# Linear attention and a two-layer MLP on one core: the preparation of the first batch is redistributed over GpSimd, VectorE and the first-layer blocks

## The chip, the core and the metric

The kernel runs on one core of a Trainium2 chip. A core has TensorE (PE, matrix products into PSUM), VectorE (DVE), ScalarE (ACT), GpSimd (POOL) and SyncE (SP, which here only issues transfers). Each engine takes its own instructions strictly in program order; GpSimd also issues the transfers that turn float32 into bf16 on the way. The metric is the device time of one execution in microseconds (us), the median of several runs.

## The reference, cut to what matters

```python
q_s = softmax over the 64 features of q;  k_s = softmax over the 576 positions of k
kv  = einsum('bhsd,bhse->bhde', k_s, v)            # 64 x 64 for each head
attn = einsum('bhsd,bhde->bhse', q_s, kv)          # 8 batches, 8 heads, 576 positions, 64 features
x = attn.transpose(0, 2, 1, 3).reshape(4608, 512)
h = x @ w_in                                       # 512 -> 2048
out = maximum(0.01 * h, h) @ w_out                 # 2048 -> 512
```

All inputs and the output are float32.

## The kernel before, in words

**Layout.** The 576 positions of a head are 64 partitions times R = 9 rows, and two heads' halves fill 128 partitions, so that a batch is a tile [128, 4, 9, 64] of `q`, `k` or `v` (HL = 4 pairs of heads; pairs 0 and 1 are called H0, pairs 2 and 3 H1). The exponentials are written as bf16 (`qe`, `ke`); v is cast to bf16 into `vb`, with a column of ones that gives the sum of k's exponentials. The product of ke and vb is `pkv`; scaled and masked it becomes `kd`, four blocks g = 0 to 3. Blocks 0 and 2 come from gg = 0 (H0), blocks 1 and 3 from gg = 1 (H1). q's exponentials are divided by their sums (`q_norm`), transposed on TensorE (`q_transpose`) and copied out of PSUM (`q_keep`) into `qT`; `attend` multiplies by kd and casts the result into `xT`, which holds x transposed in four blocks of 128 features. Row r of q gives the 64 columns from 64 r of a batch.

**The MLP.** The 4608 tokens go in nine tiles of 512. For a tile, layer 1 makes 16 units j (128 hidden features each), each with four matmuls over xT's blocks in the order 0, 2, 1, 3 (`layer1`, line 456); `leaky` (line 467) on ScalarE takes them out of PSUM into `gj`. Layer 2 (`layer2`, line 478) adds up the 16 units over four sub-tiles of 128 tokens. In tile 0 layer 1 is cut in two halves of 256 columns, two units to a PSUM bank, and layer 2 runs unit by unit, four matmuls each.

**The order.** The tile framework schedules nothing by itself here: the program's text is the order on every engine. Work of a later batch is hung in by hand: `at(t, u, ...)` puts functions behind unit u of tile t, and `run(t, u)` calls them. In tile 0 the numbers 0 to 31 are the layer-1 units of the two halves, and from 32 on the units of layer 2; so (0,41) is behind unit 9 of layer 2. PSUM has eight banks: six in the pool `psB` (units, transposes, products, all under one tag) and two in `psO`. A bank is free again when the last reader of its former tile is done.

**The start, batch 0** (lines 515 to 576). SyncE issues q's rows 0 to 3 (RA), k in two halves, v in two halves, and q's rows 4 to 8. GpSimd waits with a one-column copy into `gate` for k's second half, then issues the first half of w_in (units 0 to 7) in four pieces, first the two of gg = 0 (blocks 0 and 2), then the two of gg = 1. `q_first` takes q's first four rows with 16 small exponentials on ScalarE. k's maximum over all positions is found with VectorE and TensorE (`k_tree`, `k_max_pe`, `k_all_dve`, `k_all_pe`) and subtracted by VectorE (`k_sub_ps`, line 362). ScalarE does k's exponentials (line 203) and both casts of v (line 213). GpSimd issues w_in's second half (line 133) behind another gate, at line 542. Then follow `kv_pair` for H0 and H1, the transposes, and `attend`. Matmuls on zeros (`wake`, line 324) keep TensorE busy in between. Rows 4 and 5 (R1) and rows 6 to 8 (R2) of q follow in layer 1, with hooks at units 3 to 17.

**Batch 1.** `hold_sync(0, ...)` makes SyncE wait for the first piece of w_in's second half and then issues k (two halves), q and v of batch 1. GpSimd waits at line 572 for k's first half and issues w_out in five pieces; `hold_sync(1, ...)` waits for w_out's units 8 to 11 and lets batch 2's loads go. The hooks of unit 15 find k's maximum on VectorE (`k_tree` line 162, `k_allmax` to line 187) and subtract it (line 195): H0 on GpSimd, H1 on VectorE. q's maximum (line 226) is subtracted on GpSimd (line 256, rows RA = 0 to 3 and RB = 4 to 8), its exponential is on ScalarE (line 264), sum and division on VectorE (lines 273 and 280). `kv(1)` stands at (0,41).

Of the kernel before, what the change touches and what calls it, by code (L numbers as in the profile page):

```python
# [25 lines left out]
def kernel(  # L26
# [57 lines left out]

    ALLH, ALLR = slice(0, HL), slice(0, R)
    RA, RB = slice(0, 4), slice(4, R)
    R1, R2 = slice(4, 6), slice(6, R)
    st = [{} for _ in range(B)]


# [58 lines left out]
    def k_tree(b, hs, steps=slice(0, 4)):  # L149
        n = hs.stop - hs.start  # L150
        ks = st[b]["k"][:, hs]
        if steps.start == 0:
            st[b]["t4"] = mx_pool.tile([P, HL, 4, D], FP32, name="t4")[:, 0:n]
        t4 = st[b]["t4"]
        t2, t1 = t4[:, :, 0:2], t4[:, :, 0]
        for o, i0, i1 in (
            (t4, ks[:, :, 0:4], ks[:, :, 4:8]),
            (t2, t2, t4[:, :, 2:4]),
            (t1, t1, t4[:, :, 1]),
            (st[b]["kmax"][:, hs], t1, ks[:, :, 8]),  # L160
        )[steps]:
            nc.vector.tensor_tensor(out=o, in0=i0, in1=i1, op=ALU.max)  # L162
# [46 lines left out]
    def v_cast(eng, b, gg):  # L209
        o = vb2[b % 2][:, :, gg, 0:128].rearrange("p r (h d) -> p h r d", h=2)  # L210
        i = st[b]["v"][:, 2 * gg : 2 * gg + 2]
        if eng is nc.scalar:
            eng.copy(out=o, in_=i)
        else:
            eng.tensor_copy(out=o, in_=i)  # L215
# [12 lines left out]
    def q_first(b, rs):  # L228

        n = rs.stop - rs.start  # L230
        st[b]["nmax"] = nmax = small_pool.tile([P, HL, n], FP32, name="nmax")
        qsum = small_pool.tile([P, n, HL], FP32, name="qsum")
        for hs in (slice(0, 2), slice(2, 4)):
            nc.vector.tensor_reduce(
                out=nmax[:, hs], in_=st[b]["q"][:, hs, rs], axis=AX.X, op=ALU.max, negate=True
            )
            for h in range(hs.start, hs.stop):
                for r in range(n):
                    nc.scalar.activation(
                        out=st[b]["qe"][:, rs.start + r, h],  # L240
                        in_=st[b]["q"][:, h, rs.start + r],
                        func=AF.Exp,
                        bias=nmax[:, h, r : r + 1],
                        accum_out=qsum[:, r, h : h + 1],
                    )
        st[b]["qsum"] = qsum

    def q_first_rec(b, rs):
        n = rs.stop - rs.start
        st[b]["qrec", rs.start] = qrec = small_pool.tile([P, n, HL], FP32, name="qrec")  # L250
        nc.vector.reciprocal(out=qrec, in_=st[b]["qsum"])

    def q_sub(eng, b, rs):
        n = rs.stop - rs.start
# [19 lines left out]
        st[b]["qrec", rs.start] = qrec = small_pool.tile([P, n, HL], FP32, name="qrec")  # L274
        nc.vector.reciprocal(out=qrec, in_=qsum)

    def q_norm(b, rs):
        n = rs.stop - rs.start
        qes = st[b]["qe"][:, rs]
        nc.vector.tensor_tensor(  # L280
            out=qes,
            in0=qes,
            in1=st[b]["qrec", rs.start].unsqueeze(3).to_broadcast([P, n, HL, D]),
            op=ALU.mult,
        )
# [80 lines left out]
    def kv_pair(b, gg):  # L366
        pkv = [psB_pool.tile([P, 130], FP32, name="pkv1", tag=BANK_TAG) for _ in range(2)]
        for r in range(R):
            for hh in range(2):
                rows = slice(hh * L, (hh + 1) * L)  # L370
                nc.tensor.matmul(
                    pkv[hh][:, 0:129],
                    lhsT=st[b]["ke"][rows, r, 2 * gg : 2 * gg + 2].rearrange("p h d -> p (h d)"),
                    rhs=vb2[b % 2][rows, r, gg, 0:129],
                    start=(r == 0),
                    stop=(r == R - 1),
                )
        st[b]["pkv", gg] = pkv
# [148 lines left out]
    k_all_pe(0, 0)  # L527
    wake(2)
    k_tree(0, H1, slice(1, 4))
    k_max_pe(0, 1)  # L530
    wake(1)
    k_sub_ps(0, 0, HA)
    k_exp(0, slice(0, 1))
    k_all_dve(0, 1)
    k_all_pe(0, 1)
    wake(5)
    k_sub_ps(0, 0, HB)
    k_exp(0, slice(1, 2))
    v_cast(nc.scalar, 0, 0)
    v_cast(nc.scalar, 0, 1)  # L540
    k_sub_ps(0, 1)
    nc.gpsimd.tensor_copy(out=gate[:, 0:1], in_=st[0]["k"][:, HL - 1, R - 1, D - 1 : D])  # L542
    load_w_in(1)
    k_exp(0, H1)
    q_first_rec(0, RA)
    q_norm(0, RA)
    kv_pair(0, 0)
    wake(4)
    q_transpose(0, 0, 4)
    kv_pair(0, 1)  # L550
    for hh in range(2):
        kd_rec(0, 0, hh)
        kd_one(nc.vector, 0, 0, hh)
    q_keep(nc.scalar, 0, 0, 4, slice(0, 4, 2))
    q_keep(nc.vector, 0, 0, 4, slice(1, 4, 2))
    attend(0, [0, 2], 0, 256, nc.scalar)
    wake(3)
    kd_rec(0, 1, 0)
    kd_rec(0, 1, 1)
    kd_one(nc.vector, 0, 1, 0)  # L560
    kd_one(nc.vector, 0, 1, 1)
    q_max(0, R1)
    q_sub(nc.gpsimd, 0, R1)
    q_max(0, R2)
    q_sub(nc.gpsimd, 0, R2)


    hold_sync(0, w_in_sb[0:1, 0, F - 128 : F])
    st[1]["k"] = load(k, 1, "k_raw", [(H0, ALLR), (H1, ALLR)])
    st[1]["q"] = load(q, 1, "q_raw", [(ALLH, ALLR)])  # L570
    st[1]["v"] = load(v, 1, "v_raw", [(ALLH, ALLR)])
    nc.gpsimd.tensor_copy(out=gate[:, 0:1], in_=st[1]["k"][:, 0, 0, 0:1])
    for j0, j1 in ((0, 2), (2, 4), (4, 8), (8, 12), (12, 16)):
        load_w_out(slice(j0, j1))
    hold_sync(1, w_out_sb[0:1, 11, 0:128])
    load_all(2)


    at(0, 3, lambda: q_exp(0, R1), lambda: q_sum(0, R1), lambda: q_norm(0, R1))
    at(0, 5, lambda: q_exp(0, R2), lambda: q_sum(0, R2), lambda: q_norm(0, R2))  # L580
    at(0, 11, lambda: q_transpose(0, 4, 2), lambda: q_keep(nc.vector, 0, 4, 2))
    at(0, 13, lambda: q_transpose(0, 6, 3), lambda: q_keep(nc.vector, 0, 6, 3))
    at(0, 15, lambda: attend(0, [0, 2], 256, 256, nc.scalar))
    at(0, 15, lambda: attend(0, [1, 3], 256, 256, nc.vector))
    at(0, 17, lambda: attend(0, [0, 1, 2, 3], 512, 64, nc.scalar))
    at(0, 15, lambda: k_begin(1), lambda: q_begin(1), lambda: k_tree(1, H0), lambda: k_tree(1, H1))
    at(0, 15, lambda: k_allmax(1), lambda: k_sub(nc.gpsimd, 1, H0), lambda: k_sub(nc.vector, 1, H1))
    at(0, 15, lambda: q_max(1, RA), lambda: q_sub(nc.gpsimd, 1, RA))
    at(0, 15, lambda: q_max(1, RB), lambda: q_sub(nc.gpsimd, 1, RB))
    at(0, 29, lambda: k_exp(1, H1))  # L590
    at(0, 31, lambda: v_cast(nc.scalar, 1, 0), lambda: k_exp(1, H0))
    at(0, 33, lambda: q_exp(1, RA), lambda: q_sum(1, RA), lambda: q_norm(1, RA))
    at(0, 33, lambda: v_cast(nc.scalar, 1, 1), lambda: q_exp(1, RB), lambda: q_sum(1, RB))
    at(0, 41, lambda: kv(1))
    at(0, 41, lambda: q_norm(1, RB), lambda: kd_make(1))
    for r0 in (0, 2):
# [52 lines left out]
        return [g_pool.tile([P, 2, TT], BF16, name="gj") for _ in range(NF // 2)]  # L649

    g_sb = g_tiles()
    begun = []
    for j in range(0, 8, 2):
        ph = psB_pool.tile([P, 2, 256], FP32, name="ph", tag=BANK_TAG)
        for i in range(2):
            layer1(j + i, ph[:, i], 0, 256, slice(0, 2), i == 0)
        begun.append(ph)
    attend(0, [1, 3], 0, 256, nc.scalar)
    for half in range(2):
        for j in range(0, NF, 2):  # L660
            part = slice(2, 4) if begun else slice(0, 4)
            ph = begun.pop(0) if begun else psB_pool.tile([P, 2, 256], FP32, name="ph", tag=BANK_TAG)
            for i in range(2):
                layer1(j + i, ph[:, i], 256 * half, 256, part, i == 0, i == 1)
                if i == 1:
                    leaky(g_sb[j // 2][:, :, 256 * half : 256 * half + 256], ph)
                run(0, 16 * half + j + i)
    pout = [psO_pool.tile([P, O], FP32, name="pout") for _ in range(2)]
    pout += [psB_pool.tile([P, O], FP32, name="pout2", tag=BANK_TAG) for _ in range(2)]
    for j in range(NF):  # L670
# [62 lines left out]
```

## Time and profile before

| what | value |
|---|---|
| runs of the kernel before | 292.87, 293.10, 293.29 us; median 293.1 |
| the profiled execution's own time | 293.27 us |
| its span, first to last instruction | 291.5 us |
| TensorE busy | 280.2 us, 96% of the span |
| VectorE, ScalarE, GpSimd busy | 50%, 51%, 29% |
| TensorE's granted clock | 1.00 |
| moved by DMA | 45.76 MB, mean 157 GB/s |
| first layer-1 matmul, tile 0 | 17.37 us |
| w_in's second half landed | 23.31 us |
| layer 2 of tile 0 begins | 36.14 us |
| kv(1) begins | 44.78 us |

Times inside the profile count from the span's start. The profile comes from one execution; its span is shorter than its time by what lies before the first and behind the last instruction. In a timeline row the first number is the start, the second the time until the last of the row's instructions ended, then engine, line and operation, the tiles as output<-input with their shapes, and in brackets the idle time before it and what ended it. The chain of waits is followed back from the end of the program to what each step waited for. "xN" counts instructions.

### The profile page before, as it was taken

The page shows a single profiled execution, that of the slowest core. Times are in us where ns is not written, and L with a number is a line of the kernel's source. Part 1 is how long each engine was busy: PE and PEld are TensorE (multiplying, and loading weights), DVE is VectorE, ACT ScalarE, POOL GpSimd, SP SyncE. Part 2 cuts the span into 40 slices and gives each one's busy share as a digit, 9 for nine tenths or more (in the row PEclk, how much of TensorE's full clock was granted, in tenths as well). Part 3 has the DMA queues.
Part 4 walks back from the last instruction along what each step waited for, and adds up shares of the span by engine and source line. Part 5 has one row for each costly group of instructions (what it writes and reads, how often), then busy time and mean ns, then how long its engine had stood idle before and what let it go on. Part 6 is the DMA issues. An engine that isn't in the chain of part 4 may idle for free.

```text
span 291.5 us, 4277 instructions
## 1 busy us (share of the span) xinstructions
PE 280.2 (96%) x1645; PEld 139.9 (48%) x1672; DVE 147.0 (50%) x244; ACT 149.7 (51%) x268; POOL 85.5 (29%) x61
## 2 busy tenths in 40 slices
PE   8697999999999999999999999999999999999995
PEld 3265845444544544454444544554455444444443
DVE  2947957896790796289276546645541200110011
ACT  4957683568168506941684339533953066017400
POOL 4545280008039208703910391029200000000000
PEclk9999999999999999999999999999999999999999
DMA  7999999597639454973299139913141310131032
GB/s 255 314 202 378 256 176 397 139 286 270 124 89 338 162 119 108 336 211 86 65 338 250 36 72 318 287 36 74 36 81 38 72 36 1 38 75 33 0 73 73
DMA packets 36580, 45.76 MB, mean 157 GB/s; under 512 B 15952, under 2 KB 19280, under 8 KB 36560
## 3 DMA queue, kind: packets, MB, share of 16 engines
q1 hardware_dynamic: 33120, 41.16, 48.4%
q0 software_dynamic: 3280, 4.20, 8.3%
q8 instruction: 13, 0.21, 0.3%
q10 hardware_dynamic: 160, 0.13, 0.1%
q14 instruction: 7, 0.06, 0.1%
HBM read 36.70 MB, written 9.44 MB: 158 GB/s over the span
## 4 chain that ended last, share of the span: by engine, by line
PE 89%; DMA 3%; DVE 1%; issue 1%; ACT 1%; POOL 1%; ACTq 0%
PE pout L479 43%; PE ph L458 41%; DMA w_in_sb<-in_moe_w_in_dram 3%; PE pkv L295 3%; PE po L446 2%; DVE k_raw L362 1%; PE psum_qt L395 1%; POOL w_in_sb L133 0%; ACT gj L467 0%; ACT xT L428 0%; PE po L418 0%; DVE out_sb L473 0%; POOL gate L542 0%; ACTq L467 0%
## 5 line engine op out<-in xcount | busy, mean ns | idle before, releaser
L479 PE MATMUL pout<-w_out_sb,gj 128*128 128x512 bf16 (+2 forms) x580 | 129.6, 373 | 0.6
L458 PE MATMUL ph<-xT,w_in_sb 128*128 128x512 bf16 (+1 forms) x626 | 126.8, 357 | 3.4 <-ACT xT L428 1.4
L467 ACT ACTIVATE gj<-ph 128x512 bf16<-128x512 f32 x144 | 82.5, 603 | 58.1 <-PE ph L458 57.5
L458 PEld LDWEIGHTS <-w_in_sb 128*128 128x128 bf16 x640 | 62.1, 98 | 64.8 <-issue 4.1
L479 PEld LDWEIGHTS <-gj 128*128 128x128 bf16 x592 | 57.0, 98 | 62.1 <-ACT gj L467 0.4
L473 DVE COPY out_sb<-pout 128x512 f32<-128x512 f32 (+1 forms) x34 | 22.7, 675 | 86.2 <-PE pout L479 80.7
L195 POOL TENSOR_TENSOR k_raw<-k_raw,kall 128x2304 f32<-128x2304 f32 (+1 forms) x6 | 29.1, 4846 | 83.5 <-DVE kall L187 56.3
L273 DVE TENSOR_REDUCE qsum<-qe 128x36 f32<-128x2304 bf16 (+4 forms) x11 | 19.8, 1799 | 37.4 <-ACT qe L264 37.4
L256 POOL TENSOR_TENSOR q_raw<-q_raw,qmax 128x2304 f32<-128x2304 f32 (+4 forms) x11 | 31.1, 2839 | 25.4 <-DVE qmax L226 25.4
L452 ACT CAST xT<-po 128x320 bf16<-128x320 f32 (+1 forms) x48 | 16.8, 402 | 41.2 <-PE po L446 41.2
L203 ACT ACTIVATE ke<-k_raw 128x2304 bf16<-128x2304 f32 (+2 forms) x11 | 17.6, 1596 | 10.3 <-POOL k_raw L195 8.6
L280 DVE TENSOR_TENSOR qe<-qe,qrec 128x2304 bf16<-128x2304 bf16 (+4 forms) x12 | 21.7, 1811 | 0.4
L226 DVE TENSOR_REDUCE qmax<-q_raw 128x36 f32<-128x2304 f32 (+4 forms) x11 | 19.4, 1789 | 0.0
L264 ACT ACTIVATE qe<-q_raw 128x2304 bf16<-128x2304 f32 (+4 forms) x11 | 16.9, 1533 | 0.8 <-POOL q_raw L256 0.8
L215 POOL CAST vb<-v_raw 128x1152 bf16<-128x1152 f32 x12 | 13.5, 1153 | 0.0
L324 PE MATMUL pout<-zero 128*128 128x512 bf16 x29 | 9.6, 470 | 1.5 <-POOL zero L101 1.3
L162 DVE TENSOR_TENSOR t<-k_raw 128x1024 f32<-128x1024 f32 (+1 forms) x10 | 10.1, 1011 | 0.5 <-DMA k_raw<-in_k_dram 0.2
L162 DVE TENSOR_TENSOR t<-t 128x256 f32<-128x256 f32 (+2 forms) x20 | 9.6, 478 | 0.7
L446 PE MATMUL po<-qX,kd 128*128 128x320 bf16 (+1 forms) x48 | 9.8, 286 | 0.0
L473 ACT COPY out_sb<-pout 128x512 f32<-128x512 f32 (+1 forms) x3 | 1.7, 563 | 14.9 <-PE pout L479 14.9
L295 PEld LDWEIGHTS <-ke 64*128 64x128 bf16 x252 | 7.2, 93 | 3.0 <-ACT gj L467 1.7
L313 DVE TENSOR_TENSOR kd<-pkv,krec 64x128 bf16<-64x128 f32 x28 | 8.1, 289 | 0.7
(57 smaller groups left out, 104.8 us busy)
## 6 DMA issues: line engine op xcount, KB each, us to landing
out_dram<-out_sb SPq DMA_DIRECT2D x70, 128.0 KB, 2.4
q_raw<-in_q_dram SPq DMA_DIRECT2D x7, 1152.0 KB, 8.4
v_raw<-in_v_dram SPq DMA_DIRECT2D x7, 1152.0 KB, 11.4
k_raw<-in_k_dram SPq DMA_DIRECT2D x6, 1152.0 KB, 6.1
k_raw<-in_k_dram SPq DMA_DIRECT2D x4, 576.0 KB, 5.7
w_in_sb<-in_moe_w_in_dram POOLq DMA_DIRECT2D x8, 256.0 KB, 6.7
w_out_sb<-in_moe_w_out_dram POOLq DMA_DIRECT2D x3, 512.0 KB, 13.2
v_raw<-in_v_dram SPq DMA_DIRECT2D x2, 576.0 KB, 7.7
```

The costliest lines, as they stand in the source:

```text
L162: nc.vector.tensor_tensor(out=o, in0=i0, in1=i1, op=ALU.max)
L195: eng.tensor_tensor(out=ks, in0=ks, in1=st[b]["kall"][:, hs].unsqueeze(2).to_broadcast([P, n, R, D]), op=ALU.subtract,)
L203: nc.scalar.activation(out=st[b]["ke"][:, :, hs].rearrange("p r h d -> p h r d"), in_=st[b]["k"][:, hs], func=AF.Exp,)
L226: nc.vector.tensor_reduce(out=m, in_=st[b]["q"][:, :, rs], axis=AX.X, op=ALU.max)
L256: eng.tensor_tensor(out=qs, in0=qs, in1=st[b]["qmax", rs.start].unsqueeze(3).to_broadcast([P, HL, n, D]), op=ALU.subtract,)
L264: nc.scalar.activation(out=st[b]["qe"][:, rs].rearrange("p r h d -> p h r d"), in_=st[b]["q"][:, :, rs], func=AF.Exp,)
L273: nc.vector.reduce_sum(out=qsum, in_=st[b]["qe"][:, rs], axis=AX.X)
L280: nc.vector.tensor_tensor(out=qes, in0=qes, in1=st[b]["qrec", rs.start].unsqueeze(3).to_broadcast([P, n, HL, D]), op=ALU.mult,)
L458: nc.tensor.matmul(ph, lhsT=w_in_sb[:, cb, j * P : (j + 1) * P], rhs=xT[:, cb, c0 : c0 + n], start=(i == 0 and first), stop=(i == NB - 1 a ...
L467: nc.scalar.activation(out=o, in_=ph, func=AF.Prelu, alpha=LEAKY_SLOPE)
L473: copy(out=out_sb, in_=pout)
L479: nc.tensor.matmul(pout, lhsT=g_sb[j // 2][:, j % 2, tsub * P : (tsub + 1) * P], rhs=w_out_sb[:, j, os], start=(j == 0), stop=(j == NF - 1),)
```

## The change

What it does, all within tile 0 and batches 0 and 1:

- Both casts of v of batch 0 go from ScalarE to GpSimd: the first behind a gate on k's maximum, ahead of w_in's second issue; the second behind it.
- q's rows 0 to 3 are normed and transposed by pairs gg. GpSimd norms gg = 0 between v's first cast and w_in's second issue; VectorE norms gg = 1 behind kd. The transposes of gg = 1 stand between blocks of layer 1 (`t0`).
- Only H0's product stands ahead of layer 1; H1's (`kv1`, with kd, R1's exponential and two products of 256 columns) stands behind the second quarter of units 0 to 7.
- Units are begun in groups of four banks, quarter by quarter: units 0 to 7 two quarters ahead, units 8 to 15 three quarters ahead, with the transposes of rows 4 to 7 (`t1`, `t2`) and the products of columns 256 to 511 (`x2`) in between.
- R2 becomes rows 6 and 7, and row 8 is R3: its transposes and copy hang at (0,35), its product at (0,38), behind units 3 and 6 of layer 2 instead of layer-1 units 13 and 17. R1's norm is on GpSimd.
- The first w_out piece is issued ahead of R2's subtract and of the wait for batch 1's k; the rest are five pieces instead of four.
- In batch 1 ScalarE's order becomes k_exp H1, k_exp H0, v_cast 0 at (0,31), and q_exp RA, v_cast 1, q_exp RB at (0,32). `wake(5)` becomes `wake(3)`, and the `wake(4)` goes.

The core of the diff:

```diff
+    def q_first_norm(eng, b, gg):
+        qes = st[b]["qe"][:, RA, 2 * gg : 2 * gg + 2]
+        eng.tensor_tensor(out=qes, in0=qes, in1=st[b]["qrec2", gg].unsqueeze(3).to_broadcast([P, RA.stop, 2, D]), op=ALU.mult)
...
+    nc.gpsimd.tensor_copy(out=gate[:, 0:1], in_=st[0]["kmax"][:, HL - 1, D - 1 : D])
+    v_cast(nc.gpsimd, 0, 0)
...
-    wake(5)
+    wake(3)
+    q_first_rec(0, 0)
+    q_first_norm(nc.gpsimd, 0, 0)
+    load_w_in(1)
+    v_cast(nc.gpsimd, 0, 1)
     k_sub_ps(0, 0, HB)
     k_exp(0, slice(1, 2))
-    v_cast(nc.scalar, 0, 0)
-    v_cast(nc.scalar, 0, 1)
+    q_first_rec(0, 1)
     k_sub_ps(0, 1)
-    nc.gpsimd.tensor_copy(out=gate[:, 0:1], in_=st[0]["k"][:, HL - 1, R - 1, D - 1 : D])
-    load_w_in(1)
     k_exp(0, H1)
-    q_first_rec(0, RA)
-    q_norm(0, RA)
     kv_pair(0, 0)
-    wake(4)
-    q_transpose(0, 0, 4)
-    kv_pair(0, 1)
...
+    q_turn_first(0, 0)
     wake(3)
+    kd_rec(0, 0, 0)
+    kd_one(nc.vector, 0, 0, 0)
+    q_keep_first(nc.vector, 0, 0)
+    kd_rec(0, 0, 1)
+    kd_one(nc.vector, 0, 0, 1)
+    q_first_norm(nc.vector, 0, 1)
+    attend(0, [0], 0, 256, nc.scalar)
+    attend(0, [2], 0, 256, nc.scalar)
     q_max(0, R1)
     q_sub(nc.gpsimd, 0, R1)
+    load_w_out(slice(0, 2))
     q_max(0, R2)
     q_sub(nc.gpsimd, 0, R2)
+    def t0():
+        q_turn_first(0, 1)
+        q_keep_first(nc.scalar, 0, 1)
+    def kv1():
+        kv_pair(0, 1)
+        for hh in range(2):
+            kd_rec(0, 1, hh)
+            kd_one(nc.vector, 0, 1, hh)
+        q_exp(0, R1)
+        for g in (1, 3):
+            attend(0, [g], 0, 256, nc.scalar)
...
+    def behind_first_units():
+        q_max(0, R3)
+        q_sub(nc.gpsimd, 0, R3)
+        nc.gpsimd.tensor_copy(out=gate[:, 0:1], in_=st[1]["k"][:, 0, 0, 0:1])
+        for j0, j1 in ((2, 4), (4, 6), (6, 8), (8, 12), (12, 16)):
+            load_w_out(slice(j0, j1))
+        hold_sync(1, w_out_sb[0:1, 11, 0:128])
+        load_all(2)
+    at(0, 0, lambda: q_sum(0, R1), lambda: q_norm(0, R1, nc.gpsimd), behind_first_units)
+    at(0, 2, lambda: q_exp(0, R2), lambda: q_sum(0, R2), lambda: q_norm(0, R2))
+    at(0, 16, lambda: q_exp(0, R3))
+    at(0, 35, lambda: q_transpose(0, 8, 1), lambda: q_keep(nc.scalar, 0, 8, 1))
+    at(0, 38, lambda: attend(0, [0, 1, 2, 3], 512, 64, nc.scalar))
...
+    at(0, 31, lambda: k_exp(1, H1), lambda: k_exp(1, H0), lambda: v_cast(nc.scalar, 1, 0))
+    at(0, 32, lambda: q_exp(1, RA), lambda: q_sum(1, RA), lambda: q_norm(1, RA))
+    at(0, 32, lambda: v_cast(nc.scalar, 1, 1), lambda: q_exp(1, RB), lambda: q_sum(1, RB))
...
+    t1 = (lambda: q_transpose(0, 4, 2), lambda: q_keep(nc.scalar, 0, 4, 2))
+    t2 = (lambda: q_transpose(0, 6, 2), lambda: q_keep(nc.vector, 0, 6, 2))
+    x2 = (
+        lambda: attend(0, [0, 2], 256, 256, nc.scalar),
+        lambda: attend(0, [1, 3], 256, 256, nc.vector),
+    )
+    for j0, parts in ((0, ((0, (t0,)), (1, (kv1,)))), (8, ((0, t1), (1, t2), (2, x2)))):
+        js = range(j0, j0 + 8, 2)
+        for j, ph in zip(js, begin(js, parts)):
+            end(j, ph, 0, slice(len(parts), 4), False)
+    for j in range(0, NF, 2):
+        end(j, psB_pool.tile([P, 2, 256], FP32, name="ph", tag=BANK_TAG), 1, slice(0, 4), True)
```

`begin` opens four banks and runs layer 1's quarters over them, with the given functions behind each quarter; `end` does the rest of a pair of units, its leaky cast and its hooks.

More of the change, by code (lines that the diff above doesn't have):

```diff
@@ L86 @@
     RA, RB = slice(0, 4), slice(4, R)
-    R1, R2 = slice(4, 6), slice(6, R)
+    R1, R2, R3 = slice(4, 6), slice(6, 8), slice(8, R)
     st = [{} for _ in range(B)]
@@ L231, in q_first @@
         st[b]["nmax"] = nmax = small_pool.tile([P, HL, n], FP32, name="nmax")
-        qsum = small_pool.tile([P, n, HL], FP32, name="qsum")
-        for hs in (slice(0, 2), slice(2, 4)):
+        for gg in range(2):
+            hs = slice(2 * gg, 2 * gg + 2)
+            st[b]["qsum", gg] = qsum = small_pool.tile([P, n, 2], FP32, name="qsum2")
             nc.vector.tensor_reduce(
@@ L236, in q_first, with q_first_rec, q_turn_first, q_keep_first @@
             )
-            for h in range(hs.start, hs.stop):
+            for h in range(2):
                 for r in range(n):
                     nc.scalar.activation(
-                        out=st[b]["qe"][:, rs.start + r, h],
-                        in_=st[b]["q"][:, h, rs.start + r],
+                        out=st[b]["qe"][:, rs.start + r, 2 * gg + h],
+                        in_=st[b]["q"][:, 2 * gg + h, rs.start + r],
                         func=AF.Exp,
-                        bias=nmax[:, h, r : r + 1],
+                        bias=nmax[:, 2 * gg + h, r : r + 1],
                         accum_out=qsum[:, r, h : h + 1],
                     )
[L246 to L251, printed above, removed]
+    def q_first_rec(b, gg):
+        st[b]["qrec2", gg] = qrec = small_pool.tile([P, RA.stop, 2], FP32, name="qrec2")
+        nc.vector.reciprocal(out=qrec, in_=st[b]["qsum", gg])
+    def q_first_norm(eng, b, gg):
+        qes = st[b]["qe"][:, RA, 2 * gg : 2 * gg + 2]
+        eng.tensor_tensor(
+            out=qes,
+            in0=qes,
+            in1=st[b]["qrec2", gg].unsqueeze(3).to_broadcast([P, RA.stop, 2, D]),
+            op=ALU.mult,
+        )
+    def q_turn_first(b, gg):
+        n = RA.stop
+        ps = psB_pool.tile([P, 2, n, L], BF16, name="psum_q2", tag=BANK_TAG)
+        for r in range(n):
+            nc.tensor.matmul(
+                ps[:, :, r],
+                lhsT=st[b]["qe"][:, r, 2 * gg : 2 * gg + 2].rearrange("p h d -> p (h d)"),
+                rhs=ident,
+                is_transpose=True,
+                start=(r == 0),
+                stop=(r == n - 1),
+            )
+        st[b]["ps2", gg] = ps
+    def q_keep_first(eng, b, gg):
+        o, i = st[b]["qT"][:, gg::2, RA], st[b]["ps2", gg]
+        if eng is nc.scalar:
+            eng.copy(out=o, in_=i)
+        else:
+            eng.tensor_copy(out=o, in_=i)
     def q_sub(eng, b, rs):
@@ L275, in q_sum, with q_norm @@
         nc.vector.reciprocal(out=qrec, in_=qsum)
-    def q_norm(b, rs):
+    def q_norm(b, rs, eng=nc.vector):
         n = rs.stop - rs.start
         qes = st[b]["qe"][:, rs]
-        nc.vector.tensor_tensor(
+        eng.tensor_tensor(
             out=qes,
@@ L535 @@
     k_all_pe(0, 1)
-    wake(5)
+    wake(3)
[3 more added lines that the diff above has]
+    v_cast(nc.gpsimd, 0, 1)
     k_sub_ps(0, 0, HB)
     k_exp(0, slice(1, 2))
-    v_cast(nc.scalar, 0, 0)
-    v_cast(nc.scalar, 0, 1)
+    q_first_rec(0, 1)
     k_sub_ps(0, 1)
-    nc.gpsimd.tensor_copy(out=gate[:, 0:1], in_=st[0]["k"][:, HL - 1, R - 1, D - 1 : D])
-    load_w_in(1)
     k_exp(0, H1)
-    q_first_rec(0, RA)
-    q_norm(0, RA)
     kv_pair(0, 0)
-    wake(4)
-    q_transpose(0, 0, 4)
-    kv_pair(0, 1)
[L551 to L556, printed above, removed]
-    wake(3)
[L558 to L561, printed above, removed]
+    q_turn_first(0, 0)
+    wake(3)
+    kd_rec(0, 0, 0)
[6 more added lines that the diff above has]
+    attend(0, [2], 0, 256, nc.scalar)
     q_max(0, R1)
     q_sub(nc.gpsimd, 0, R1)
+    load_w_out(slice(0, 2))
     q_max(0, R2)
     q_sub(nc.gpsimd, 0, R2)
+    def t0():
[9 more added lines that the diff above has]
+            attend(0, [g], 0, 256, nc.scalar)
     hold_sync(0, w_in_sb[0:1, 0, F - 128 : F])
@@ L571 @@
     st[1]["v"] = load(v, 1, "v_raw", [(ALLH, ALLR)])
[L572 to L585, printed above, removed]
-    at(0, 15, lambda: k_begin(1), lambda: q_begin(1), lambda: k_tree(1, H0), lambda: k_tree(1, H1))
-    at(0, 15, lambda: k_allmax(1), lambda: k_sub(nc.gpsimd, 1, H0), lambda: k_sub(nc.vector, 1, H1))
-    at(0, 15, lambda: q_max(1, RA), lambda: q_sub(nc.gpsimd, 1, RA))
@@ L589 @@
[L589 to L593, printed above, removed]
+    def behind_first_units():
[6 more added lines that the diff above has]
+        load_all(2)
@@ new lines @@
+    at(0, 0, lambda: q_sum(0, R1), lambda: q_norm(0, R1, nc.gpsimd), behind_first_units)
[3 more added lines that the diff above has]
+    at(0, 38, lambda: attend(0, [0, 1, 2, 3], 512, 64, nc.scalar))
+    at(0, 15, lambda: k_begin(1), lambda: q_begin(1), lambda: k_tree(1, H0), lambda: k_tree(1, H1))
+    at(0, 15, lambda: k_allmax(1), lambda: k_sub(nc.vector, 1, H1), lambda: k_sub(nc.gpsimd, 1, H0))
@@ L594 @@
+    at(0, 16, lambda: q_sum(0, R3), lambda: q_norm(0, R3))
+    at(0, 16, lambda: q_max(1, RA), lambda: q_sub(nc.gpsimd, 1, RA))
+    at(0, 16, lambda: q_max(1, RB), lambda: q_sub(nc.gpsimd, 1, RB))
+    at(0, 31, lambda: k_exp(1, H1), lambda: k_exp(1, H0), lambda: v_cast(nc.scalar, 1, 0))
+    at(0, 32, lambda: q_exp(1, RA), lambda: q_sum(1, RA), lambda: q_norm(1, RA))
+    at(0, 32, lambda: v_cast(nc.scalar, 1, 1), lambda: q_exp(1, RB), lambda: q_sum(1, RB))
     at(0, 41, lambda: kv(1))
@@ L651, with begin, end @@
     g_sb = g_tiles()
[L652 to L667, printed above, removed]
+    def begin(js, parts):
+        phs = [psB_pool.tile([P, 2, 256], FP32, name="ph", tag=BANK_TAG) for _ in js]
+        for i, between in parts:
+            for j, ph in zip(js, phs):
+                for h in range(2):
+                    layer1(j + h, ph[:, h], 0, 256, slice(i, i + 1), h == 0, False)
+            for fn in between:
+                fn()
+        return phs
+    def end(j, ph, half, part, first):
+        for h in range(2):
+            layer1(j + h, ph[:, h], 256 * half, 256, part, first and h == 0, h == 1)
+            if h == 1:
+                leaky(g_sb[j // 2][:, :, 256 * half : 256 * half + 256], ph)
+            run(0, 16 * half + j + h)
+    t1 = (lambda: q_transpose(0, 4, 2), lambda: q_keep(nc.scalar, 0, 4, 2))
[3 more added lines that the diff above has]
+        lambda: attend(0, [1, 3], 256, 256, nc.vector),
+    )
+    for j0, parts in ((0, ((0, (t0,)), (1, (kv1,)))), (8, ((0, t1), (1, t2), (2, x2)))):
[4 more added lines that the diff above has]
+        end(j, psB_pool.tile([P, 2, 256], FP32, name="ph", tag=BANK_TAG), 1, slice(0, 4), True)
     pout = [psO_pool.tile([P, O], FP32, name="pout") for _ in range(2)]
```

## The prediction, made before the changed kernel was run

> **What bounds the kernel now.** The page's first lines come first: TensorE is busy 96% of the span, so only its idle time and its order at the start can be worth anything.
>
> ```profile
> PE 280.2 (96%) x1645; PEld 139.9 (48%) x1672; DVE 147.0 (50%) x244; ACT 149.7 (51%) x268; POOL 85.5 (29%) x61
> ```
>
> The chain of waits, in order of time, then shows where another engine holds it up (columns: start, length, what):
>
> ```profile
> 14.94 8.36 DMA w_in_sb<-in_moe_w_in_dram
> 23.31 0.14 issue
> 23.44 1.69 PE ph L458 x14
> ...
> 27.75 0.60 ACT gj L467
> 28.35 0.48 ACT xT L428
> ...
> 30.03 6.11 PE ph L458 x56
> ...
> 36.41 8.37 PE pout L479 x38
> 44.78 1.13 PE pkv L295 x36
> ```
>
> The reader is to see that w_in's second half lands at 23.31, that TensorE then has work except about 1.1 us (ACT gj, ACT xT), and that layer 2 runs without a hole from 36.14 to kv(1) at 44.78. Ten units of layer 2, four matmuls of 0.216 us each, lie ahead of kv(1), so unit j=8 begins at 44.78 - 8 x 0.216 = **43.05**. From there both kernels have the same work; I compare that moment.
>
> Batch 1's preparation is the second thread. The timelines of VectorE, GpSimd and ScalarE (start, length, instruction):
>
> ```profile
> 28.80 0.68 DVE L162 TENSOR_TENSOR t<-k_raw 128x512 f32<-128x512 f32 x1
> ...
> 30.63 0.69 DVE L162 TENSOR_TENSOR t<-k_raw 128x512 f32<-128x512 f32 x1
> ...
> 34.29 0.45 DVE L187 STREAM_TRANSPOSE kall<-m 128x256 f32<-128x256 f32 x1
> ...
> 34.89 3.74 POOL L195 TENSOR_TENSOR k_raw<-k_raw,kall 128x1152 f32<-128x1152 f32 x1 [5.95 <-DVE kall L187]
> 38.60 4.18 POOL L256 TENSOR_TENSOR q_raw<-q_raw,qmax 128x1024 f32<-128x1024 f32 x2
> ...
> 38.76 1.16 ACT L203 ACTIVATE ke<-k_raw 128x1152 bf16<-128x1152 f32 x1
> 40.53 1.06 ACT L264 ACTIVATE qe<-q_raw 128x1024 bf16<-128x1024 f32 x1 [0.61 <-POOL q_raw L256]
> 41.49 1.14 ACT L213 CAST vb<-v_raw 128x1152 bf16<-128x1152 f32 x1
> 42.82 1.27 ACT L264 ACTIVATE qe<-q_raw 128x1280 bf16<-128x1280 f32 x1 [0.18 <-POOL q_raw L256]
> ```
>
> It ends with q_exp(1,RB) on ScalarE at 44.09, and nothing on TensorE waits for that now: batch 0's row 8 was already multiplied at 29.91.
>
> The DMA view in windows shows the engines saturated from 3 us to 41 us (share 1.0 or more), with 200 GB/s written while a float32-to-bf16 load runs and 390 while a plain one runs; where both run (29 to 32.5) each queue has about half. So bytes that are put ahead push back those behind.
>
> **The change, part by part.** Times are in the profiled execution's clock.
>
> 1. *v's casts leave ScalarE.* Two casts of 1.14 us go to GpSimd (1.153 us each by row L215). ScalarE's H1 exponential then starts when VectorE's subtract ends, at 13.45 (two reciprocals of 0.2 us go ahead of it, while one of 0.24 and the 1.22 us norm go behind or away), and not at 14.45. On GpSimd: gate at 10.85, cast 11.05 to 12.2, then q's first pair. A bf16 512-element multiply on GpSimd is not in the trace; the float32 subtract of 512 took 1.044 us. Bounds: 0.55 (the 512-element memset) and 1.5 (that subtract x 3.74/2.53, see 4); I take 1.05, since it too has two inputs. So w_in's second issue starts at 13.25 against 13.20, and with 1.5 at 13.7. The second cast stands behind it, 15.85 to 17.0.
>
> 2. *The first product comes earlier.* kv_pair(0,0) waits no longer for ScalarE's cast (12.35 to 13.5) but for its exponential, 12.7 against 13.54. Then 0.68 to 13.4, four transposes (half of 0.61) to 13.75, VectorE's kd and a copy (0.35 + 0.42) to 14.4, the matmul and a 256-column cast of 0.37 to 15.15. w_in's first two pieces (issued 8.28 and about 8.95, 6.1 and 6.3 to landing) are there at 15.2. The first layer starts at about **15.25 instead of 17.37**.
>
> 3. *But the middle is given back.* The second pair's product needs GpSimd's second cast (17.0), four kd operations on VectorE (1.0), and two casts of 0.37 on ScalarE behind q_exp(0,R1), which waits for GpSimd's q_sub (17.0 + 1.04). The second half of the contraction of units 0 to 7 starts at about 19.75 (before: 20.16). Units 8 to 15 then run three of four quarters ahead, between 21.35 and 24.6: w_in's pieces for the third landed at 23.31. The hole of 1.15 us at 22.3 is filled, the 1.1 us behind 27.75 goes, and what was left after 23.44 shrinks: 8 matmuls of quarter three (0.86), the four products for columns 256 to 511 (0.45), quarter four (0.86) and 64 matmuls of the second half (6.9). From 23.7 that makes 32.8; layer 2 begins at **33.0 instead of 36.14**, 3.1 us earlier. Row 8's transposes and products (0.1 + 0.12) now lie inside layer 2. With no further wait j=8 would begin at 33.0 + 6.9 + 0.2 = 40.1. The leaky casts, 0.5 us apart, finish at 27.6 and are not in the way.
>
> 4. *Row 8 behind.* Its product stands behind unit 6 of layer 2, and its copy out of PSUM is a **ScalarE** instruction issued behind unit 3, after everything that unit 0 put on ScalarE: v_cast(1,1) and q_exp(1,RB). So TensorE, in order, waits for the end of batch 1's thread. When is that? VectorE is free for k_tree at 25.9 (product 24.8 to 25.1, cast 0.69). The second half of k lands later than now: the trace has it at 20.48 + 6.3 = 26.8, and the w_out piece that is moved ahead (issued at 18.1, right behind w_in in GpSimd's queue) puts 512 KB into the stretch from 22.3 on. At half share that lasts 2.6 us and delays k by 1.15, to 27.95. So the second tree starts at 28.0 (30.63 before); kall 4.11 later, as before: 32.1. GpSimd's subtract 3.74, plus 0.36 for row 8's norm on VectorE, ends at 36.3. ScalarE then has, in its new order, k_exp, v_cast, q_exp RA, v_cast, q_exp RB: 1.15 + 1.1 + 1.05 + 1.1 + 1.25 to 41.9 (GpSimd's q_sub, 36.3 + 1.9 + 2.3 = 40.5, is just in time), then the 256-element copy, 0.36 by the row of 0.366: **42.2**. TensorE came there at 33.0 + 7 x 0.864 + 0.1 = 39.1: it stands about 3 us. Then the products (0.12) and unit 7 (0.86): j=8 at 43.2, against 43.05.
>
> The 0.36 comes from a row: the subtract of 1152 elements took 3.74 beside VectorE's own subtract of 1.36, where half of the 2304-element one (5.068) is 2.53; so a VectorE operation with two inputs in SBUF seems to stop GpSimd for most of its length (zero at the other end).
>
> [...]
>
> 5. *w_out in six pieces.* Bytes ahead of units 8 to 11 are the same and the engines are full, so they land at 40.6 as now (the issue that waits for them starts at 40.62). That is behind 40.1 but ahead of 43.2: it costs nothing under the wait of part 4, and 0.5 if that wait were gone. The extra issue, 0.75 us, is done by 29.7, ahead of kall. R1's norm on GpSimd (1.05) ends by 21.0; TensorE wants it at 22.4.
>
> **Sum.** 3.1 us won before layer 2, about 3.0 lost at row 8's product, 0.2 of row 8's work moved behind: +0.15. The profiled execution took 293.27, 0.17 over the median: 293.4 on it, **293.3** as a median.
>
> **Rivals.**
> - *The thread is late (slower).* Every microsecond by which k's second half or w_in's last pieces land later comes out one for one at row 8's product; it counts as slower from a kall at 32.55. For: GpSimd's multiply may take its upper 1.5, w_in's issue then slips by 0.45; k may get less than half a share. Against: w_in's ring was not empty at 13.3. +0.6 to +1.5, about 294.2. Chance 0.30.
> - *The clock drops in the hole (slower).* The first zero matmuls went at 0.427 us for 4.3 us, and 0.216 later; a second such stretch would cost half of 4.3, 2.1: 295.4. For: no hole in the trace is as long as 3 us. Against: after the 1.15 us hole at 22.3, 14 matmuls took 1.69 us, full speed. Chance 0.08. [...]
> - *The thread is early (faster).* If the w_out piece delays k by nothing and VectorE is free at 25.5 (w_in 23.31 + 0.86 + 0.45 + 0.7 and hand-overs), kall is at 31.45: -0.6 to -0.9, 292.4. Chance 0.12.
> - *Row 8 doesn't wait* (the change does what a reading without the queue order promises). Then w_out binds j=8 at 40.65: -2.4, 290.9. Against: ScalarE's order is fixed by the hooks. Chance 0.06.
>
> **Numbers.** Forecast 293.3, itself 292.7 to 293.9, chance 0.44. 0.2% (0.6 us) is about what a measurement of this kernel can tell from no change. Faster 0.12 + 0.06 = 0.18, slower 0.30 + 0.08 = 0.38. The range 292.2 to 294.9 leaves out the last rival, the clock and thin ends.
>
> **What would show it.** First layer-1 matmul near 15.3; layer 2 near 33; a hole of 2 to 4 us on TensorE ahead of the 64-column products, ended by ScalarE's copy of row 8; j=8 within 0.6 of 43.05; k_raw's second piece landing near 28. No hole, or a hole while w_out's unit 8 is what is waited for, would make it wrong; so would a clock below 1.00 behind it.

## The result and the profile after

| kernel | median of its executions, us | ratio to the kernel before, 95% interval |
|---|---|---|
| before | 293.13 (292.87 to 293.29, 4) | |
| changed | 296.69 (296.08 to 297.74, 4) | 1.0124 [1.0104, 1.0143] |

The changed kernel is 3.6 us slower; 293.3 had been forecast, and the range ended at 294.9. Two executions in these studies were disturbed (303.77 us of the kernel before, with a mean clock of 0.949, and 600.74 of an experiment) and are left out everywhere.

The changed kernel's page first: busy times, and the granted clock in 40 slices of the span, in tenths.

```profile
span 294.4 us, 4302 instructions
PE 282.4 (96%) x1666; PEld 139.8 (47%) x1666; DVE 147.8 (50%) x247; ACT 148.7 (51%) x271; POOL 91.0 (31%) x67
...
PEclk9999998999999999999999999999999999999999
```

TensorE is busy for 2.2 us more than before, and the clock has an 8 in the seventh slice (44.2 to 51.5 us), where the kernel before had only nines. The TensorE timeline of the changed kernel (start, length, instruction; in brackets the idle time ahead and what ended it):

```profile
15.11 1.03 PE L488 MATMUL ph<-xT,w_in_sb 128*128 128x256 bf16 x8 [0.38 <-DMA w_in_sb<-in_moe_w_in_dram]
...
32.85 1.89 PE L509 MATMUL pout<-w_out_sb,gj 128*128 128x512 bf16 x8
34.97 1.89 PE L509 MATMUL pout<-w_out_sb,gj 128*128 128x512 bf16 x8 [0.23 <-DMA w_out_sb<-in_moe_w_out_dram]
...
36.81 2.75 PE L509 MATMUL pout<-w_out_sb,gj 128*128 128x512 bf16 x12
43.39 0.37 PE L448 MATMUL po<-qT,kd 128*128 128x64 bf16 x4 [3.83 <-ACT qT L440]
43.57 4.19 PE L509 MATMUL pout<-w_out_sb,gj 128*128 128x512 bf16 x12
47.70 1.20 PE L325 MATMUL pkv<-vb,ke 64*128 64x129 bf16 x36
```

The first layer starts at 15.1 and layer 2 at 32.85, as forecast. In the same view of the kernel before layer 2 starts at 35.98, so it is 3.1 us ahead (the 36.14 of the table is the end of the last first-layer matmul; here that is 33.02). Then TensorE stands for 3.83 us ahead of row 8's product, until ScalarE's copy (L440). Behind it twelve matmuls take 4.19 us; the twelve ahead took 2.75. kv(1) begins at 47.70 instead of 44.71: 3.0 us, and the span is 2.9 us longer. So the whole loss lies ahead of kv(1). The granted clock by stretches says why the twelve are slow (columns: stretch, its length, busy time of PE, PEld, DVE, ACT, POOL, granted clock, DMA share, GB/s):

```profile
38.00:40.00 2.00, 1.56 (x8) 0.59 (x6) 0.90 (x1) 0.81 (x2) 2.00 (x2) 1.00 1.24 206
40.00:42.00 2.00, 0.00 (x0) 0.00 (x0) 1.29 (x2) 1.81 (x3) 1.77 (x1) 1.00 0.83 128
42.00:44.00 2.00, 0.61 (x6) 0.33 (x6) 1.97 (x3) 1.54 (x3) 0.00 (x0) 0.77 0.92 265
44.00:46.00 2.00, 2.00 (x6) 0.72 (x5) 1.93 (x3) 0.17 (x1) 0.00 (x0) 0.50 0.95 363
46.00:48.00 2.00, 2.00 (x19) 0.85 (x19) 0.68 (x1) 0.00 (x0) 0.00 (x0) 0.88 1.04 412
```

The clock is 0.50 in the stretch behind the hole, and from the three stretches below 1.00 ((1 - 0.77) + (1 - 0.50) + (1 - 0.88), each times 2 us and over 0.5) it was so for about 3.4 us. Stretches of 0.1 us place it from 43.07 to 46.49 us. The chain of waits names what led to the late copy (start, length, what):

```profile
32.25 1.36 DVE k_raw L196
33.60 0.34 DVE qsum L303
...
34.18 0.04 DVE qe L310
34.22 2.08 issue
36.30 1.22 DVE qmax L227
...
37.59 4.20 POOL q_raw L286 x2
...
41.81 1.27 ACT qe L294
43.08 0.27 ACT qT L440
```

VectorE reaches row 8's norm (L310) at 34.18 and the next maximum only at 36.30: "issue" is time in which it waited for nothing that the profile shows. The timelines of VectorE and GpSimd show what that time is:

```profile
34.18 2.19 DVE L310 TENSOR_TENSOR qe<-qe,qrec 128x256 bf16<-128x256 bf16 x1
...
32.36 3.73 POOL L196 TENSOR_TENSOR k_raw<-k_raw,kall 128x1152 f32<-128x1152 f32 x1 [1.79 <-DVE kall L188]
37.59 4.18 POOL L286 TENSOR_TENSOR q_raw<-q_raw,qmax 128x1024 f32<-128x1024 f32 x2 [1.50 <-DVE qmax L227]
```

The norm of 256 elements has a length of 2.19 us, where 512 elements took 0.69 at 22.33. GpSimd's subtract of k ran from 32.36 to 36.09, and the norm ended 0.28 us behind it. Then GpSimd itself stood for 1.50 us, because VectorE's first maximum of q came behind the norm; and ScalarE's last exponential, ahead of row 8's copy, waited for GpSimd.

### The profile page after: what moved, and what is told of

Same layout as the page of the kernel before. It is cut to its first block, busy times and chain, and to the rows that moved or that the text cites. A ratio compares the mean times of both kernels' runs of the same rounds, so it can differ in the third digit from the quotient of the medians.

```text
span 294.4 us, 4302 instructions
## 1 busy us (share of the span) xinstructions
PE 282.4 (96%) x1666; PEld 139.8 (47%) x1666; DVE 147.8 (50%) x247; ACT 148.7 (51%) x271; POOL 91.0 (31%) x67
## 4 chain that ended last, share of the span: by engine, by line
PE 84%; DMA 6%; DVE 3%; POOL 3%; issue 1%; ACT 1%; SPq 1%; DVEq 0%
PE pout L509 41%; PE ph L488 38%; DMA k_raw<-in_k_dram 4%; PE pkv L325 3%; DMA w_in_sb<-in_moe_w_in_dram 2%; PE po L476 2%; POOL q_raw L286 1%; DVE t L163 1%; POOL w_in_sb L134 1%; DVE k_raw L196 0%; ACT qe L294 0%; DVE qmax L227 0%; PE psum_qt L425 0%; POOL vb L216 0%; PE po L448 0%
## 5 line engine op out<-in xcount | busy, mean ns | idle before, releaser
L509 PE MATMUL pout<-w_out_sb,gj 128*128 128x512 bf16 (+2 forms) x592 | 132.2, 376 | 0.2 <-DMA w_out_sb<-in_moe_w_out_dram 0.2
L310 DVE TENSOR_TENSOR qe<-qe,qrec 128x2304 bf16<-128x2304 bf16 (+4 forms) x11 | 21.7, 1971 | 0.4
L216 POOL CAST vb<-v_raw 128x1152 bf16<-128x1152 f32 x14 | 15.8, 1155 | 0.0
L354 PE MATMUL pout<-zero 128*128 128x512 bf16 x24 | 8.3, 483 | 1.3 <-POOL zero L101 1.3
```

The lines of the kernel that those rows point to most:

```text
L310: eng.tensor_tensor(out=qes, in0=qes, in1=st[b]["qrec", rs.start].unsqueeze(3).to_broadcast([P, n, HL, D]), op=ALU.mult,)
L509: nc.tensor.matmul(pout, lhsT=g_sb[j // 2][:, j % 2, tsub * P : (tsub + 1) * P], rhs=w_out_sb[:, j, os], start=(j == 0), stop=(j == NF - 1),)
```

## The experiments

Two questions were open: whether the hole, its length and the clock are the whole loss, and why the norm stood. The ratios below are each against the kernel before on the same chip (293.27 to 293.34 us); the chips differ from one set of experiments to the next.

**1. The product of row 8 late.**

```diff
-    at(0, 38, lambda: attend(0, [0, 1, 2, 3], 512, 64, nc.scalar))
+    at(0, 45, lambda: attend(0, [0, 1, 2, 3], 512, 64, nc.scalar))
```

> The product of row 8 hangs behind unit 13 of layer 2 instead of unit 6; all else as changed. Theory (TensorE waits in order for ScalarE's copy of row 8, and that wait with the slow clock behind it is the whole loss): no hole at unit 7, clock 1.00, layer 2 goes on until w_out's units 8 to 11 (landed by 40.0) and then waits 0.4 to 0.9 us at batch 1's transposes for q's norm (43.4, 46.7): 290.5 to 291.8 us, faster than before. Rival (w_out's order or its six pieces hold layer 2): the hole moves to another w_out unit and the time stays at 293 or more.

292.03 us, 0.996 [0.9945, 0.9975]. The hole at unit 7 is gone and w_out holds nothing there; kv(1) begins at 42.12. TensorE waited 0.7 us at batch 1's later transposes, behind a VectorE thread that the norm had pushed back; that wait was expected, and why the time missed its window by 0.2 us stays open. One line moved takes 4.7 us off the changed kernel, so the wait and what hangs on it are more than the whole loss.

**2. The hole filled with matmuls on zeros.**

```diff
+    def fill(n):
+        ps = psB_pool.tile([P, TT], FP32, name="fill", tag=BANK_TAG)
+        for i in range(n):
+            nc.tensor.matmul(ps, lhsT=zero[:, 0:P], rhs=zero, start=(i == 0), stop=(i == n - 1))
-    at(0, 38, lambda: attend(...))
+    at(0, 38, lambda: fill(12), lambda: attend(...))
```

> Twelve matmuls on zeros (2.6 us) stand ahead of row 8's product, into a bank of their own. Theory (3.83 us of idle TensorE let the clock fall, and units 7 to 9 ran at half speed): the hole ends at the same 43.4, the clock stays at 1.00 and the 12 matmuls behind it take 2.6 instead of 4.2 us: 1.5 to 2.2 us faster than the changed kernel, 294.5 to 295.2. Rival (the slow matmuls wait for w_out or for PSUM): 4.2 us again, 296 to 297.

294.79 us, 1.0054 [1.0039, 1.0069]. Its TensorE timeline:

```profile
39.74 2.75 PE L631 MATMUL fill<-zero 128*128 128x512 bf16 x12
43.56 0.28 PE L448 MATMUL po<-qT,kd 128*128 128x64 bf16 x4 [1.07 <-ACT qT L440]
43.67 2.75 PE L509 MATMUL pout<-w_out_sb,gj 128*128 128x512 bf16 x12
46.36 1.20 PE L325 MATMUL pkv<-vb,ke 64*128 64x129 bf16 x36
```

Row 8's product comes no earlier (43.56), and the twelve matmuls behind it take 2.75 us again. Useless work made the kernel 1.9 us faster; the rival that the twelve waited for w_out or PSUM falls.

**3. The norm behind batch 1's maxima on VectorE.**

```diff
-    at(0, 16, lambda: q_sum(0, R3), lambda: q_norm(0, R3))
     at(0, 16, lambda: q_max(1, RA), lambda: q_sub(nc.gpsimd, 1, RA))
     at(0, 16, lambda: q_max(1, RB), lambda: q_sub(nc.gpsimd, 1, RB))
+    at(0, 16, lambda: q_sum(0, R3), lambda: q_norm(0, R3))
```

> On VectorE the sum and norm of row 8 stand behind the two maxima of batch 1's q instead of ahead. Theory (the norm stood 1.9 us because GpSimd's subtract holds what both need, and pushed the maxima and all of ScalarE's thread back): the maxima end at 36.1, the copy of row 8 at 42.0, the hole is 2.7 us or split in two, clock 1.00: 293.0 to 293.7. The norm itself is again long (until about 38.0) if GpSimd's next subtract began first, and 0.4 us if what it waited for was only data: then the time is much the same, but the norm's length tells the two apart. Rival (the thread is held elsewhere): the copy stays at 43.

293.45 us, 1.0013 [1.0003, 1.0023], clock 0.998 or more in all ten executions. VectorE and GpSimd:

```profile
36.76 1.55 DVE L310 TENSOR_TENSOR qe<-qe,qrec 128x256 bf16<-128x256 bf16 x1
...
36.13 4.37 POOL L286 TENSOR_TENSOR q_raw<-q_raw,qmax 128x1024 f32<-128x1024 f32 x2
```

The norm stands again, now until 38.31, beside GpSimd's next subtract, which had begun at 36.13. That harms nobody but TensorE's transposes of row 8: the hole is split into 1.47 and 0.88 us. The copy ends at 42.06, and the time is 0.15 us from the one that had been forecast for the change. GpSimd's first subtract of q (1.89 us) ended at 38.02, and the norm again 0.29 us behind it.

**4 and 5. The norm with its factors in PSUM.** The reciprocals are written to a PSUM bank, so that the multiply has one input in SBUF:

```diff
+        st[b]["qrec", rs.start] = qrec = psB_pool.tile([P, n, HL], FP32, name="qrecp", tag=BANK_TAG)
...
-    at(0, 16, lambda: q_sum(0, R3), lambda: q_norm(0, R3))
+    at(0, 16, lambda: q_sum_ps(0, R3), lambda: q_norm(0, R3))
```

> The norm of row 8 stays where the change put it, but its factors (the reciprocals) lie in PSUM, so that the VectorE multiply has one input in SBUF instead of two. Theory (the multiply stood because GpSimd, in its subtract, holds the second way into SBUF): the norm takes about 0.4 instead of 2.19 us beside the same subtract, the maxima of q end at 37.2, the copy of row 8 at 42.1, the hole is 2.6 us, clock 1.00: 293.1 to 293.7. Rival (any VectorE multiply into SBUF, or a wait for data, stands behind GpSimd): 2.2 us again and 296 to 297.

296.46 us, 1.0092 [1.0061, 1.0123]. The norm did as expected, and the time did not: the bank given to the reciprocals was the next one in turn for a first-layer unit, and TensorE stood 3.3 us for it in layer 1. The waits of this kernel:

```profile
PE ph L488 <- DVE qe L310: 3.3, 1, 3.3
```

The second try takes the bank behind unit 30 (`at(0, 30, ...)` for these hooks and the two maxima), with the order on every engine unchanged.

> The norm of row 8 with its factors in PSUM again, but its bank is taken behind unit 30 of layer 1 and not behind unit 16, so that no first-layer unit is given that bank; the order on each engine is the same as in the first try. Theory: the norm takes 0.42 us beside GpSimd's subtract as in the first try, layer 2 begins at 33.0, the copy of row 8 ends at 42.2 and the hole is 2.6 us, clock 1.00: 293.2 to 293.8. Rival (the slow clock needs no more than such a hole): a stretch at 0.50 and 295 or more.

293.34 us, 1.002 [0.9999, 1.0041]; ten executions, two of them at 295.0 and 295.8 with a mean clock of 0.993 and 0.994. VectorE and GpSimd:

```profile
34.57 0.42 DVE L310 TENSOR_TENSOR qe<-qe,qrecp 128x256 bf16<-128x256 bf16 x1 [0.26 <-DVE qrecp L636]
34.91 2.61 DVE L227 TENSOR_REDUCE qmax<-q_raw 128x16 f32<-128x1024 f32 x2
...
32.45 3.73 POOL L196 TENSOR_TENSOR k_raw<-k_raw,kall 128x1152 f32<-128x1152 f32 x1 [1.78 <-DVE kall L188]
```

The same multiply beside the same subtract takes 0.42 us instead of 2.19. So neither data nor VectorE as such had held it, but its second input in SBUF. The maxima (one input) were not held either: 2.61 us here, the first of them beside the subtract, and 2.60 in the changed kernel, where GpSimd stood during the first. The copy of row 8 ended at 41.95, against 43.34 in the changed kernel. Two things were not as expected: the hole was 1.90 us instead of 2.6, as TensorE came to it later (layer 2 began at 33.14 and waited 0.48 us for w_out), and the clock fell in two executions.

**6. The w_out piece back behind k.** `load_w_out(slice(0, 2))` goes from the start to the head of the loop behind the gate.

> The first w_out piece goes back behind the gate on batch 1's k. Theory (the piece costs VectorE 0.3 us of waiting at k's first half, landing at 26.2): k lands near 24.6, the tree starts at 25.9, the hole ends at 43.1 and is still over 3.4 us long; w_out's first units land at 33 to 35 and hold layer 2 by 0.3 us: 295.8 to 296.7. Rival (the piece ahead of k is the main loss): the tree starts at 25, the hole ends at 42 and the clock stays up: 293.5 to 294.5.

294.72 us, 1.0065 [1.0039, 1.009]. The gate on k's first half opens at 24.9 instead of 26.3 and the tree starts at 25.79 instead of 26.20; the hole is 3.09 us and ends at 42.96. The profiled execution and three others kept the clock (294.3 to 294.8); two lost it (296.2, 296.6; 0.992). The time fell between the two windows: the piece costs 0.4 us of the thread, and about 1.5 us more only where it tips the clock. Behind k it costs TensorE 0.56 us of waiting for w_out (0.3 had been expected).

**7. A shorter fill, twice.** `fill(4)` in place of `fill(12)`.

> The changed kernel with 4 instead of 12 matmuls on zeros ahead of row 8's product: TensorE's idle time is cut from 3.8 to about 2.9 us, its end stays at 43.4. [...]

296.13 us, 1.009 [1.0065, 1.0115]. Of four executions two were at 294.7 and 295.1 (clock 1.00, 0.998), as with twelve matmuls (294.79), and two at 296.1 and 296.4 (0.994, 0.993). No profile shows either pair, so it was run again:

> The kernel with 4 matmuls on zeros once more, for a profile and more executions: in the first try 2 of 4 fell to a mean clock of 0.993 or 0.994. [...] Rival (the first try was disturbed): one group at 294.5 to 295.2.

296.44 us, 1.012 [1.0084, 1.0156], not one group but three: 294.66 and 294.82 (clock 1.00), 296.17 and 296.70 (0.994, 0.992), and one that the first try did not have, 298.01 and 298.68 (0.987). The profiled execution, one at full clock, has the hole at 3.06 us:

```profile
39.38 1.03 PE L631 MATMUL fill<-zero 128*128 128x512 bf16 x4
43.47 0.28 PE L448 MATMUL po<-qT,kd 128*128 128x64 bf16 x4 [3.06 <-ACT qT L440]
43.58 2.75 PE L509 MATMUL pout<-w_out_sb,gj 128*128 128x512 bf16 x12
```

**8 and 9. Row 8 without a wait.** One kernel hangs all of row 8 at the end of layer 2 (transposes and copy at (0,45), product at (0,47), norm as in experiment 3). The other undoes the part: R2 is again rows 6 to 8, `t2` transposes three rows, and the product stands behind unit 17.

```diff
-    R1, R2, R3 = slice(4, 6), slice(6, 8), slice(8, R)
+    R1, R2 = slice(4, 6), slice(6, R)
-    at(0, 38, lambda: attend(0, [0, 1, 2, 3], 512, 64, nc.scalar))
+    at(0, 17, lambda: attend(0, [0, 1, 2, 3], 512, 64, nc.scalar))
```

> Row 8's transposes and copy hang at (0,45), its product at (0,47), its norm on VectorE behind batch 1's maxima. Theory (without the wait the 3.1 us won ahead of layer 2 stay, up to w_out's landing at 40.0 for unit 8): no hole over 0.5 us in layer 2, 290.4 to 291.2. Rival (w_out or batch 1's thread binds at once): 292 or more, as with the late product alone.

> Undoes one part: rows 6 to 8 are again one group, row 8's transposes stand with theirs between the first-layer blocks and its product behind unit 17; all else as changed. Theory: layer 2 begins at 33.3, no hole at unit 7, batch 1's thread 0.8 us earlier than in the changed kernel for the lack of row 8's norm and more for the lack of its stand: 290.4 to 291.2. Rival (the loss is in another part, the casts on GpSimd or w_out's order): 293 or more.

Row 8 last: 291.26 us, 0.9918 [0.9891, 0.9945], 0.06 over its window. Row 8 back: **291.03 us, 0.9913 [0.9881, 0.9944]**, the lowest median here, below both kernels (the two intervals overlap). Its TensorE timeline:

```profile
33.66 8.80 PE L509 MATMUL pout<-w_out_sb,gj 128*128 128x512 bf16 x39
42.39 1.20 PE L325 MATMUL pkv<-vb,ke 64*128 64x129 bf16 x36
```

Layer 2 runs without a hole to kv(1), which begins 2.3 us ahead of before (44.71), and the time is 2.3 us shorter. So the change's other parts are together a gain. Putting row 8 behind lets layer 2 begin 0.8 us earlier (32.85 for 33.66) and makes the kernel 5.7 us slower on balance (296.69 for 291.03).

**10. On top of row 8 back, the w_out piece behind k.**

> As the kernel with row 8 back, and the first w_out piece behind the gate on k again. Theory: k lands 1.4 us earlier, which nothing waits for now, and layer 2 waits 0.5 us for its first w_out piece (33.6): 0.2 to 0.5 us slower than with row 8 back alone. Rival (k's landing binds): faster by 0.3.

291.45 us, 0.9927 [0.9902, 0.9953]. The median is 0.4 us above that of row 8 back, as much as was expected, but inside the two intervals, and TensorE's waits name none for w_out: layer 2 begins 0.22 us later (33.88) because the first layer did (15.50 for 15.28). So the expected cause was not seen.

**11. On top of row 8 back, v's casts on ScalarE again.**

> The kernel with row 8 back, and with both casts of v on ScalarE as before. Theory (the casts give an earlier first product, but w_in's landing and the second quarter's wait give it back): the first layer starts 1.0 to 1.8 us later, layer 2 begins 0 to 0.8 us later, 291.0 to 291.9. Rival (the casts carry the gain): layer 2 begins 1.5 us later and 292.5 or more.

291.58 us, 0.9945 [0.993, 0.9961]. The first layer starts at 15.95 (15.28 with the casts on GpSimd), layer 2 at 34.34 (33.66). The first number is less late than expected (0.67 us, not 1.0 to 1.8), the others fit: the casts are worth about 0.5 us, between medians of two chips.

## Why the prediction was wrong, point by point

**Two terms failed: the 0.36 us for row 8's norm in the sum, and the clock behind the hole, which the sum put at nothing.** The first alone would have left the time inside the range (293.3 + 1.2 = 294.5); the second took it out.

- *The earlier product, the middle given back, layer 2 at 33.0* (parts 1 to 3): right. First layer 15.11 (forecast 15.25), the rest of units 0 to 7 from 19.70 (19.75), units 8 to 15 begun from 21.4 on, layer 2 at 32.85. GpSimd's multiply took 1.08 (1.05), which is 1.6 times VectorE's 0.69 for as many elements.
- *Row 8's product waits for ScalarE's thread* (part 4, the mechanism): right, the wait was named with its instruction and its place.
- *Its end*: wrong by 1.2 us, 43.39 for 42.2. **The step that failed first is the term of 0.36 us for row 8's norm.** The row behind it (a subtract of 3.74 beside a VectorE subtract) showed GpSimd waiting, because VectorE had begun 0.12 us earlier (34.77 and 34.89). I priced the next meeting in the same direction. But here GpSimd's subtract had begun, and VectorE stood: 1.9 us, on the engine that the whole thread goes through. GpSimd's subtract itself lost nothing (32.36 to 36.09, 3.73 us against 3.74 before), but its next one began at 37.59, where the sum had 36.3. Experiment 3 takes the norm out of the thread and meets the forecast time; experiment 5, with one input in PSUM, shows the cause (0.42 us for 2.19, the copy at 41.95 for the forecast 42.2). In both traces the one that began later was the one that stood: VectorE here, for 1.9 us (from its start at 34.18 to the subtract's end at 36.09), and GpSimd in the forecast's row, for about 1.2 us (3.74 less 2.53).
- *The clock rival*, at a chance of 0.08 and left out of the range: it happened in all four executions, by the mean clock of 0.986 to 0.994. **This is the second step that failed, and the larger one.** In the profiled execution it cost 1.5 us, from kv(1) at 47.70 against 46.36 - (43.56 - 43.39) = 46.19 in experiment 2; 2.1 had been estimated. With the hole filled and the norm still held, the time was 294.79, inside the range. My reason against it (full speed behind a hole of 1.15 us) said nothing about one of 3 us and more, and I had the hole itself too short. The clock fell in 4 of 4 executions at 3.83 us of idle time and in 6 of 10 at 3.06 us, but also in 2 of 10 of a kernel whose profile has 1.90 us, so these runs show no sharp limit.
- *The sum*: forecast for the profiled execution 293.4; add 1.2 and 1.5 and it is 296.1, measured 296.22. The median, 296.69, is higher because two of the four executions had a still lower mean clock (0.986 and 0.987).
- *The thread is late* by k's landing: k's first half landed at 26.2, 0.3 us behind VectorE being free, and the second half was no wait. The second tree began at 28.11 (forecast 28.0) because the first one had begun late, not by the wait that was forecast: the number was right by another path, which is luck. The kall time was 32.2 (forecast 32.1). Not the cause.
- *Row 8 doesn't wait*: not the case. Its price, 290.9, is near what the kernel with row 8 back takes (291.03), but that is luck: the price had w_out binding unit 8, and no wait for w_out is seen there.
- *w_out under the wait*: right; units 8 to 11 had landed by 40.0, and the one wait for w_out was 0.23 us.

Open: the executions with a mean clock of 0.986 or 0.987 (297.2, 297.7 and, with four matmuls of fill, 298.0, 298.7) would fit two stretches at half clock, by an estimate from the one of 3.4 us that a profile caught (1.5 us each on the 294.79 of experiment 2 is 297.8); no profile caught a second, so whether and where it lies isn't shown. Nor did a profile catch the two executions at 0.993 and 0.994 of the norm from PSUM, second try, so that their low clock is put down to the 1.90 us by argument only.

## What to carry to other kernels

When work is moved behind something, walk its copy and its norm through the queues of the engines that issue them: the product sat in a good place on TensorE, and its copy behind six long ScalarE instructions of the next batch. Where a VectorE instruction with two SBUF inputs met a long GpSimd subtract here (two SBUF inputs too), the one that came second paid: VectorE 1.9 us in the changed kernel, GpSimd about 1.2 us in the kernel before. Take the order of starting from the timelines, and keep the first kind (or its second input) off a thread that others wait for. A hole on TensorE like those behind which the clock fell here (3.06 to 3.83 us, 16 of 25 executions; perhaps 1.90 us, 2 of 10) should be priced with a stretch at half clock behind it, 1.5 us in the profiled execution, and with a spread between executions. Filling it (294.79 us), splitting it (293.45) or moving the waiting instruction further back (292.03) each helped here, against 296.69.

## What the runs showed of the hardware

- In the profile that caught it the half clock began 0.3 us ahead of the hole's end (43.07 and 43.39 us) and held for 3.4 us, 3.1 of them in work. By the length of TensorE's idle time (from the one profile of each kernel; the other executions' idle times were not seen), executions with a mean clock of 0.994 or less:

| kernel | idle, us | executions with the low clock |
|---|---|---|
| changed | 3.83 | 4 of 4 |
| norm from PSUM, first try | 3.31 (in layer 1) | 4 of 5 |
| w_out behind k | 3.09 | 2 of 6 |
| 4 matmuls of fill, both runs | 3.06 | 6 of 10 |
| norm from PSUM, second try | 1.90 | 2 of 10 |
| norm behind the maxima | 1.47 and 0.88 | 0 of 10 |
| 12 matmuls of fill | 1.07 | 0 of 4 |

- It is a matter of the execution, not of the kernel alone: 3.09 us left the clock up in four executions and not in two. The five kernels without such a hole (experiments 1 and 8 to 11, 24 executions; no wait over 0.73 us in their profiles from 16 us on) never showed it; the kernel before, with 1.15 us at 22.3, showed it once in the 50 executions beside the experiments.
- VectorE's multiply of 256 elements with both inputs in SBUF, begun during a GpSimd subtract, ended 0.28 us behind the subtract in the changed kernel (36.37 and 36.09; length 2.19 us) and 0.29 us behind it in experiment 3 (38.31 and 38.02; 1.55 us). With one input in PSUM it took 0.42 us beside the same subtract (experiment 5).
